# Linear attention and a bilinear feed-forward layer on one core: blocks of 128 tokens of all four rows instead of 256 tokens of two rows

## The chip, the cores and the metric

The kernel runs on one core of one Trainium2 chip. The time is device microseconds of one execution; the median of several is compared. Lower is better. "The profile" is the record of one execution by the hardware profiler, "the trace" is what it holds of single instructions, and `L787` is line 787 of the kernel before. Engines: PE is TensorE (PEld its weight loads), DVE is VectorE, ACT is ScalarE, POOL is GpSimd, SP is SyncE, which here only issues DMAs.

## The reference

For each of 4 rows and 8 heads a state of 48x48 runs over 768 tokens; each channel of the state decays by `alpha`. Its output goes through a bilinear feed-forward layer.

```python
q, k, v, alpha: (4, 8, 768, 48) float32, alpha in 0.8 to 1.0
state = np.zeros((B, H, D, D))
for t in range(S):
    state = alpha[:, :, t, :, None] * state + einsum('bhd,bhe->bhde', k[:, :, t], v[:, :, t])
    y[:, :, t] = einsum('bhd,bhde->bhe', q[:, :, t], state)
x = y.transpose(0, 2, 1, 3).reshape(3072, 384)
a = x @ w_a                 # (384, 1536)
b = x @ w_b
out = (a * b) @ w_out       # (1536, 384)
```

## The kernel before

**Blocks.** The work is cut into six blocks ("chunks", class `Chunk`), each of 512 tokens. Block `c` holds two rows (`b0 = c % 2 * 2`) and 256 tokens of each (segment `s = c // 2`). Its tiles put a pair of neighbouring tokens on a partition (`r` is which of the two), so 64 partitions are 128 tokens: `g` is the half of the partitions, the first or second 128 tokens, and `u` is which of the block's two rows.

**Steps of a block.** Each has a short name, which the table `OPS` at the end of the kernel maps to a function:

- `ld` (L519) loads alpha, keys, queries, values; the last argument names the issuing engine (Y is SP, P is POOL, S is ACT, V is DVE). `W` (L501) and `Wo` (L504) load the weights as bfloat16 through POOL. A load or step of `0a` or `0b` takes four of the eight heads of row `u` = 0.
- `ln` takes logarithms of alpha on ACT; `l2` (L533, DVE) adds the two tokens of each pair; `A` (L552) forms prefix sums over partitions by one fp32 matmul with a triangular matrix `ut`. Later blocks use `H`, `L` and `A2` (L572) for the same sum in two pieces. `E` (L594, ACT) takes exponentials of the sums with both signs (`beta`, `invb`).
- As the sums are for pairs, the first token of a pair has to be levelled: `ra` (L579, ACT) and `lv` (L586) multiply first-token keys by alpha and first-token queries by its inverse. `mk` and `mq` (L600, DVE) multiply keys and queries by the exponentials into `QKp`.
- `C` (L643) transposes by PE, `Ce` evicts the transposed tile; blocks 2 to 5 use the DMA transpose `T` (L654) instead. `D` (L709) makes scores, `M` (L714, DVE) masks them, or `Mc` (L718, ACT) copies and `Mm` (L722, DVE) masks. `v` casts values.
- `K` (L680) makes the update of the state on PE, `dk` and `de` (L622, L628) or `dr` and `dl` give the decay over a half, `k` (L694 to L698, DVE) applies both. `S0` holds states between segments, `Sm` those between the two halves of a segment.
- `SB` and `SA` add what the carried state gives to the output (L733, `carried`), `Y` adds the tokens within the block (L733, `inner`), `X` (L768) evicts the result as the feed-forward's input.
- Feed-forward: `a` and `b` (L787) for one of 12 slices of 128 and for a half (`0`, `1`) or all (`*`) of the block; `as` (L793) evicts `a` on ACT, `pr` (L801) multiplies on DVE, `o` (L809) and `oc` (L820) make the output, `ot` and `otc` evict, `st` and `stc` store.
- `fill` (L543) runs matmuls of zeros whose result nobody reads. `cu`, `ci`, `cm`, `cz`, `cs`, `c1`, `c1a` set up constants: triangular matrix, identity, masks, zero padding, zero states, ones, and ACT's function table.

**What sets the order.** All is written out by hand in the string `PROGRAM`: `0: ld a 0a Y` is step `ld` of block 0 with its arguments. Each engine runs its instructions in that order, and a DMA is issued in its issuing engine's order. The last number of many steps is the PSUM bank, eight in all; steps that name the same bank wait for each other. The loaded tiles and work tiles of a name have two buffers (`bufs`) or as many as is said.

Of the kernel before, what the change touches and what calls it, by code (L numbers as in the profile page):

```python
# [17 lines left out]
0: cu; ci; c1a; ld a 0a Y; cm 1; cz 0 q P; cs 1 0 P; c1; ld a 0b Y; fill 7 1; ld a 1 Y; ln 0a; cu2 P; ld q 0b P; ra 0a; fill 1 2; ln 0b; c2 P; ld v 0 P; ld v 1 P  # L18
0: l2 0a V; ld k 0b Y; A 0a 5; l2 0b V; ld q 1 P; ld q 0a Y; cs 0 m P; cm 0; E 0a b; ld k 0a Y; W b 0 256; ld k 1 Y; ra 0b; E 0a i; ln 1; fill 10 3; W a 256 768
0: cz 1 v V; l2 1 V; cz 0 b V; lv 0a q V; dk 3; A 0b 1; mq 0a V; fill 2 0; lv 0a k V; cs 0 0 V; mk 0a V; lv 0b k V; lv 1 k P; A 1 2; E 0b i; E 1 i; E 0b b  # L20
0: mk 0b V; de; E 1 b; C 0 0 5; lv 0b q V; v 0 S; fill 5 7; Ce 0 0 V; ra 1; D 0 0 2; mq 0b V; C 0 1 7; W a 0 256; M 0 0; K 0 0 0; Ce 0 1 S; fill 5 2; k 0 0 V
0: mk 1 V; SB 0 4; D 0 1 2; lv 1 q V; v 1 S; Mc 0 1; mq 1 V; Mm 0 1 V; K 1 1 6; K 1 0 7; k 1 0 V; K 0 1 1; C 1 0 0; Ce 1 0 S; cz 0 v P; Y 0; k 1 1 V; SA 0
0: X 0 S; k 0 1 V; W b 256 768
1: ld a 0 P; ld a 1 P
0: W a 768 1536; C 1 1 3; Ce 1 1 S; D 1 0 6; a 1 0 1; a 5 0 5; b 1 0 4; a 4 0 3; as 1 0; M 1 0; as 5 0; SB 1 6; D 1 1 1; a 3 0 5; W b 768 1536
1: ld k 0 P; ld q 0 P
0: as 4 0; b 5 0 3; pr 1 0; M 1 1; a 2 0 0; pr 5 0; cz 1 b P; as 3 0; b 2 0 4; b 4 0 5; pr 4 0
1: ld v 0 P
0: Wo 0 6; SA 1; Y 1; as 2 0; X 1 S
1: ld k 1 P  # L30
0: b 3 0 2; a 0 0 1; b 0 0 0; b 1 1 6; as 0 0; pr 2 0; pr 3 0; a 1 1 2
1: ln 0
0: a 2 1 4; b 0 1 5; a 4 1 1; as 1 1; b 4 1 7; pr 1 1; pr 0 0; as 2 1
1: ln 1
0: b 2 1 6; a 3 1 4; a 0 1 0; a 10 * 3
1: ra 0; l2 0 V
0: pr 2 1
1: l2 1 V
0: a 5 1 6; as 4 1; as 0 1
1: H 0 V  # L40
0: b 5 1 0
1: dk 1
0: as 5 1; Wo 6 12; pr 4 1; pr 5 1; a 9 * 6; b 11 * 0; cs 1 m P
1: lv 0 k P; H 1 S; ra 1; ld q 1 P; lv 0 q P
0: pr 0 1
1: L 0 V
0: as 10 *; cz 1 q V
1: de; A2 0 7
0: b 10 * 1
1: L 1 V  # L50
2: ld a * P
0: a 11 * 5; as 9 *; as 3 1; pr 10 *
1: A2 1 2
0: b 9 * 3; as 11 *; b 3 1 5
1: E 0 b; E 0 i
# [27 lines left out]
2: ln *  # L83
1: SA 0; Y 0
2: l2 * V
1: k 1 0 V
2: H * S
1: X 0 S; M 1 0; k 1 1 V
0: ot 0 S
# [866 lines left out]
```

## Time and profile before

| | |
|---|---|
| time, median of 3 runs | 199.71 us (198.07 to 200.48) |
| time of the profiled execution | 199.88 us |
| its span, first to last instruction | 197.8 us |
| PE busy | 188.0 us, 95% |
| DVE busy | 134.6 us, 68% |
| ACT busy | 106.0 us, 54% |
| POOL busy | 51.9 us, 26% |
| read from HBM, written | 25.98 MB, 4.74 MB |
| feed-forward matmuls (L787), busy | 56.2 us with w_b, 56.0 us with w_a |
| output matmuls (L809), busy | 49.4 us |

The profiled execution took 199.88 us, of which 197.8 us are its span. Busy times are sums per engine; an engine that is idle while another sets the end costs nothing. The clock that TensorE was granted stands at full speed in all slices of the page. The page's 40 slices are 4.9 us each; the DMA engines move 212 to 269 GB/s in slices 2 to 10 and 21 GB/s in slice 12.

### The profile page before, as it was taken

Reading aid. Unit: us, or ns where it says so; the run is one execution under the profiler, and the core shown is the slowest. Engines: PE = TensorE matmul, PEld = TensorE weight load, DVE = VectorE, ACT = ScalarE, POOL = GpSimd, SP = SyncE. Lnnn points to the kernel's source line nnn. Section 1 sums busy time; section 2 is a strip of 40 time slices with the busy share of each in tenths; the row PEclk is TensorE's granted clock in tenths of the full one; section 3 lists DMA queues with packets and bytes.
Section 4 is the critical chain, followed back from the end, with each engine's and each line's share of the span. In section 5 each row is a group of like instructions: output and inputs, shape, how many; then the busy total and the mean of one; then the engine's idle time right before and its main releaser. Section 6 shows DMA issues by size and latency. Waiting matters only on the chain.

```text
span 197.8 us, 6031 instructions
## 1 busy us (share of the span) xinstructions
PE 188.0 (95%) x2591; PEld 115.2 (58%) x2608; DVE 134.6 (68%) x223; ACT 106.0 (54%) x194; POOL 51.9 (26%) x70
## 2 busy tenths in 40 slices
PE   7877999999999999899999999999999999999993
PEld 2435886466788876644556644557555454545562
DVE  1599858886999989569778499955777524364311
ACT  5357686755699753196356566544435652334020
POOL 7989717681020206500005527000000000000000
PEclk9999999999999999999999999999999999999999
DMA  5999999999926999995999969500259100000224
GB/s 137 254 224 212 245 257 217 264 259 269 215 21 156 142 224 286 187 259 130 207 242 206 121 167 220 77 0 0 42 73 259 50 3 0 0 0 3 80 80 159
DMA packets 60282, 29.40 MB, mean 149 GB/s; under 512 B 51144, under 2 KB 58184, under 8 KB 60256
## 3 DMA queue, kind: packets, MB, share of 16 engines
q0 software_dynamic: 18688, 14.35, 40.4%
q1 hardware_dynamic: 41424, 14.57, 33.7%
q8 instruction: 20, 0.33, 0.7%
q10 hardware_dynamic: 144, 0.10, 0.2%
q14 instruction: 6, 0.05, 0.1%
HBM read 25.98 MB, written 4.74 MB: 155 GB/s over the span
## 4 chain that ended last, share of the span: by engine, by line
PE 83%; DMA 6%; DVE 5%; issue 2%; SPq 1%; ACT 1%; DVEq 0%; ACTq 0%
PE psum L787 42%; PE psum L809 23%; PE psum L733 7%; PE psum L709 4%; DMA kqT<-QKp 3%; DMA k_t<-in_k_dram 3%; PE psum L680 2%; PE psum L572 2%; DVE QKp L600 1%; SPq L519 1%; PE psum L643 1%; PE psum L820 1%; DVE prod L801 1%; DVE m L714 1%; PE psum L543 1%
## 5 line engine op out<-in xcount | busy, mean ns | idle before, releaser
L787 PE MATMUL psum<-xT,wb_t 128*128 128x512 bf16 (+1 forms) x264 | 56.2, 336 | 0.4 <-issue 0.2
L787 PE MATMUL psum<-xT,wa_t 128*128 128x512 bf16 (+1 forms) x261 | 56.0, 335 | 0.6 <-issue 0.2
L809 PE MATMUL psum<-wo_t,prod 128*128 128x384 bf16 x276 | 49.4, 326 | 0.1
L787 PEld LDWEIGHTS <-wb_t 128*128 128x128 bf16 x270 | 25.6, 98 | 19.3 <-issue 0.7
L809 PEld LDWEIGHTS <-prod 128*128 128x128 bf16 x276 | 26.2, 98 | 18.4 <-issue 0.2
L787 PEld LDWEIGHTS <-wa_t 128*128 128x128 bf16 x270 | 25.6, 98 | 19.1 <-issue 0.2
L718 ACT ACTIVATE m<-psum 128x1024 bf16<-128x1024 f32 x15 | 15.0, 1022 | 12.4 <-PE psum L709 12.4
L586 POOL TENSOR_TENSOR k_t<-k_t,a_t 128x384 f32<-128x384 f32 x8 | 8.5, 1064 | 40.2 <-issue 24.2
L600 DVE TENSOR_TENSOR QKp<-q_t,beta 128x768 bf16<-128x768 f32 (+1 forms) x13 | 12.2, 935 | 5.2 <-issue 2.9
L586 POOL TENSOR_TENSOR q_t<-q_t,ra 128x384 f32<-128x384 f32 x7 | 7.9, 1126 | 28.1 <-ACT ra L579 12.1
L824 ACT ACTIVATE ot<-psum 128x384 f32<-128x384 f32 (+1 forms) x13 | 6.1, 479 | 16.9 <-PE psum L809 14.4
L826 DVE COPY ot<-psum 128x384 f32<-128x384 f32 (+1 forms) x12 | 6.3, 535 | 10.6 <-PE psum L809 9.2
L768 ACT ACTIVATE xT<-psum 128x768 bf16<-128x768 f32 x9 | 7.3, 808 | 10.9 <-PE psum L733 10.8
L722 DVE TENSOR_TENSOR m<-m,mask 128x1024 bf16<-128x1024 bf16 x15 | 11.2, 748 | 1.8 <-ACT m L718 1.8
L714 DVE TENSOR_TENSOR m<-psum,mask 128x1024 bf16<-128x1024 f32 x9 | 11.0, 1221 | 1.3 <-PE psum L709 1.2
L600 DVE TENSOR_TENSOR QKp<-k_t,invb 128x768 bf16<-128x768 f32 (+1 forms) x13 | 11.4, 886 | 0.1
L733 PE MATMUL psum<-m,vx 64*64 64x128 bf16 x576 | 10.5, 217 | 1.1 <-DVE m L722 0.6
L526 ACT ACTIVATE la<-a_t 128x1536 f32<-128x1536 f32 (+2 forms) x9 | 9.5, 1058 | 2.7 <-DMA a_t<-in_alpha_dram 2.7
L709 PE MATMUL psum<-kqT 64*64 64x128 bf16 x384 | 9.9, 219 | 1.1 <-DVE kqT L651 0.9
L733 PEld LDWEIGHTS <-vx 64*64 64x64 bf16 x576 | 9.0, 107 | 2.2 <-issue 2.1
L543 PE MATMUL psum<-wz 128*128 128x512 bf16 x28 | 8.5, 440 | 1.8 <-DVE one L455 1.2
L533 DVE TENSOR_TENSOR l<-la 128x768 f32<-128x768 f32 (+2 forms) x9 | 6.2, 686 | 5.6 <-ACT la L526 5.6
(252 smaller groups left out, 278.8 us busy)
## 6 DMA issues: line engine op xcount, KB each, us to landing
out_dram<-ot SPq DMA_DIRECT2D x23, 192.0 KB, 3.1
a_t<-in_alpha_dram POOLq DMA_DIRECT2D x3, 768.0 KB, 9.8
q_t<-in_q_dram POOLq DMA_DIRECT2D x3, 768.0 KB, 11.5
k_t<-in_k_dram SPq DMA_DIRECT2D x3, 768.0 KB
v_t<-in_v_dram POOLq DMA_DIRECT2D x4, 384.0 KB, 8.7
q_t<-in_q_dram POOLq DMA_DIRECT2D x3, 384.0 KB, 9.7
wo_t<-in_moe_w_out_dram POOLq DMA_DIRECT2D x2, 576.0 KB, 15.2
v_t<-in_v_dram POOLq DMA_DIRECT2D x4, 192.0 KB, 8.8
```

Of the source, the lines that this page charges most:

```text
L526: nc.scalar.activation(out=ch.la[:, us, hs].rearrange("p b h r d -> p (b h r d)"), in_=ch.a[:, us, hs].rearrange("p b h r d -> p (b h r d) ...
L543: nc.tensor.matmul(bank(i), lhsT=wz[:, :C], rhs=wz, start=True, stop=True)
L586: eng.tensor_mul(x, x, by)
L600: eng.tensor_mul(QKp[ch.c % 2][:, u, j, :, hs, :D], src[:, u, hs].rearrange("p h r d -> p r h d"), by[:, u, hs].rearrange("p (o h) d -> p ...
L709: nc.tensor.matmul(s2[g * HC:(g + 1) * HC, r, p, rk, :], lhsT=ch.kqT[u][rs, 1, rk, 2 * h + p, g * HC:(g + 1) * HC], rhs=queriesT(ch, u, 2 ...
L714: nc.vector.tensor_mul(m.rearrange("p r a k s -> p (r a) (k s)"), ch.s2[u, h].rearrange("p r a k s -> p (r a) (k s)"), maskn(4))
L718: nc.scalar.activation(out=m.rearrange("p r a k s -> p (r a) (k s)"), in_=ch.s2[u, h].rearrange("p r a k s -> p (r a) (k s)"), func=AF.Copy)
L722: eng.tensor_mul(x, x, maskn(4))
L733: nc.tensor.matmul(y[c * DP:(c + 1) * DP, g, j // 2 * C:(j // 2 + 1) * C], lhsT=lhsT, rhs=rhs, start=(g, c) not in begun, stop=False, skip ...
L768: nc.scalar.activation(out=o_, in_=i_, func=AF.Copy)
L787: nc.tensor.matmul(p, lhsT=(wa_t, wb_t)[w][:, kk, f * 128:(f + 1) * 128], rhs=ch.xT[:, kk, us, :], start=(kk == 0), stop=(kk == KT - 1))
L809: nc.tensor.matmul(op, lhsT=ch.prod[:, f, at:at + C], rhs=wo_t[:, f, :], start=(f == 0), stop=(f == NFF - 1))
```

## The change

A block now holds 128 tokens of all four rows. `g` is a pair of rows (rows `2g` and `2g+1`) and `u` which of the two, so the two partition halves are different rows at the same tokens, and block `c` follows block `c-1` in every row. `Sm` is gone, and block 0 has no carried state, so its `Y` opens the output tile itself. A load covers one half of the partitions and its last argument says which; the two halves of a tile are loaded by two instructions, in part from two queues, and ACT issues loads too.

In block 0, `B` (`cum_both`) replaces `l2`, `ra`, `lv` and `A`: PE forms the prefix sums of both tokens of a pair by four fp32 matmuls, with `ut` and a shifted triangular matrix `uts`; the exponentials are taken for both tokens and lie in the buffer that the feed-forward's products use later. `dk` multiplies by a two-column matrix `og` in place of `one`, so that one matmul serves both halves. The order of the whole program is new.

The diff, cut to its core:

```diff
 PROGRAM = """
-0: cu; ci; c1a; ld a 0a Y; cm 1; cz 0 q P; cs 1 0 P; c1; ld a 0b Y; fill 7 1; ld a 1 Y; ln 0a; cu2 P; ld q 0b P; ra 0a; fill 1 2; ln 0b; c2 P; ld v 0 P; ld v 1 P
-0: l2 0a V; ld k 0b Y; A 0a 5; l2 0b V; ld q 1 P; ld q 0a Y; cs 0 m P; cm 0; E 0a b; ld k 0a Y; W b 0 256; ld k 1 Y; ra 0b; E 0a i; ln 1; fill 10 3; W a 256 768
...
+0: ld a 0a S 0; cm 0; cz 0 q V; c1; cz 0 b P; ld k 0a Y 0; ld a 0b S 1; ld q 0b P 0; cu; ci; ld k 0b P 1; ld a 0a Y 1; cz 1 q V; ld a 0b Y 0; ld k 0a S 1
+0: cu2 V; ld q 0a Y 1; ld q 0a S 0; cz 0 v P; cm 1; c1a; ld k 0b S 0; ld q 0b S 1; ld v 0 P 1; cus; fill 6 6; ld a 1 S 1; ln 0a; ld a 1 S 0; B 0a 6; ld q 1 Y 0
+0: ld k 1 S 1; ln 0b; ld v 0 P 0; ld k 1 Y 0; E 0a i; E 0a b; ld q 1 Y 1; B 0b 2; E 0b b; mk 0a V; ld v 1 P 0; E 0b i; W a 0 256; fill 5 0; mq 0a V; ld v 1 P 1
+0: mq 0b V; C 0 0 2; W b 0 256; mk 0b V; Ce 0 0 V; dk 0 4; C 0 1 5; W a 256 768; ln 1; D 0 0 0; B 1a 2; de 0; Ce 0 1 S; D 0 1 6; M 0 0; B 1b 4; E 1a b; M 0 1
+0: E 1a i; E 1b i; v 0 V
+1: ld a 1 P 0
+0: W b 256 768
+1: ld a 0 P 0; ld a 1 P 1; ld a 0 P 1
+0: E 1b b; mk 1a V; mk 1b V; Y 0 6; K 0 0 1; mq 1b V; X 0 S; k 0 0 V; mq 1a V; dk 1 2; W a 768 1536; C 1 1 5; a 1 0 3; Ce 1 1 V; C 1 0 6; v 1 S; Ce 1 0 V
+0: a 0 0 7; b 0 0 4; D 1 1 0; as 0 0; D 1 0 6; pr 0 0; as 1 0; M 1 1; Mc 1 0; Mm 1 0 V; b 1 0 3; a 4 0 5; a 3 0 4; a 5 0 0; as 4 0; de 1; pr 1 0; K 0 1 2
+0: Y 1 5; W b 768 1536; b 4 0 7; as 5 0; b 3 0 0; k 0 1 V; X 1 S; as 3 0; pr 3 0; b 2 0 1
...
-    one = cst.tile([C, 1], F32, name="one")
+    og = cst.tile([C, 2], F32, name="og")
+    uts = cst.tile([C, C], F32, name="uts")
-    Sm = [cst.tile([C, 2, D + P2 * VS], BF16, name=f"Sm{i}") for i in range(2)]
...
+    def const_uts():
+        x, y = (t.rearrange("p (g s) -> p g s", g=2) for t in (uts, ut))
+        nc.vector.memset(x[:, :, 0:1], 0.0)
+        nc.vector.tensor_copy(x[:, :, 1:], y[:, :, :HC - 1])
...
-    def load(ch, what, us, eng):
+    def load(ch, what, us, g, eng):
...
-        eng.dma_start(out=t[:, us, hs].rearrange("p b h r d -> p (b h) (r d)"),
-                      in_=src[ch.b0 + us.start:ch.b0 + us.stop, hs, ch.s * 2 * C:(ch.s + 1) * 2 * C, :].rearrange("b h (p r) d -> p (b h) (r d)", r=2))
+        eng.dma_start(out=t[g * HC:(g + 1) * HC, us, hs].rearrange("p b h r d -> p (b h) (r d)"),
+                      in_=src[2 * g + us.start:2 * g + us.stop, hs, ch.c * C:(ch.c + 1) * C, :].rearrange("b h (p r) d -> p (b h) (r d)", r=2))
...
+    def cum_both(ch, uh, i):
+        u, hs = uh[0].start, uh[1]
+        n = (hs.stop - hs.start) * D
+        ch.pf[u, hs.start, hs.stop] = p = wide(i)[:, :, :n]
+        x = ch.la[:, u, hs]
+        for r in range(2):
+            nc.tensor.matmul(p[:, r], lhsT=ut, rhs=x[:, :, 0, :], start=True, stop=False)
+            nc.tensor.matmul(p[:, r], lhsT=ut if r else uts, rhs=x[:, :, 1, :], start=False, stop=True)
...
     def expo(ch, uh, what):
...
+        if ch.c == 0:
+            if not hasattr(ch, "invb"):
+                x = wk.tile([128, NFF, NT], BF16, name="prod").rearrange("p f n -> p (f n)").bitcast(F32).rearrange("p (w u h r d) -> p w u h r d", w=2, u=2, h=H, r=2)
+                ch.invb, ch.beta = x[:, 0], x[:, 1]
...
-    def decay_pe(ch, tag):
+    def decay_pe(ch, us, tag):
...
+                xs = [ch.la[:, u, hd, rk, :] for rk in range(2)] if ch.c == 0 else [ch.l2[:, u, hd, :]]
+                for n, x in enumerate(xs):
+                    nc.tensor.matmul(s2[r * DP:r * DP + D, e:e + 2], lhsT=x, rhs=og, start=(n == 0), stop=(n == len(xs) - 1))
...
     def state(ch, us, g, eng):
-        old, mid, new = cut(S0[ch.s % 2], rows), cut(Sm[i], us), cut(S0[(ch.s + 1) % 2], rows)
-        src, dst = ((old, mid), (mid, new))[g]
+        rows = slice(2 * g + us.start, 2 * g + us.stop)
+        src, dst = cut(S0[ch.c % 2], rows), cut(S0[(ch.c + 1) % 2], rows)
...
-        row = (ch.b0 + m % 2) * S + (2 * ch.s + m // 2) * C
-        return out[row:row + C, :]
+        return out[m * S + ch.c * C:m * S + (ch.c + 1) * C, :]
...
-        "Y": lambda x, u: inner(x, int(u)),
+        "Y": lambda x, u, t=None: (t and out_tile(x, int(u), t), inner(x, int(u))),
```

In the later blocks the loads by half go out from POOL (42 loads in all, 23 before) and SP, block 1's four `lv` run on DVE where they ran on POOL, `K` and `k` are done for blocks 0 to 4 and not for block 5, and steps stand in other places and banks. At the end of the program both halves of the last output tile are evicted by ACT.

## The prediction

> **What bounds the kernel now** ("now" is the kernel before throughout). I first cut the span at the first feed-forward (FF) matmul and at the last matmul (windows over all engines: busy time and count of PE, PEld, DVE, ACT, POOL, then clock, DMA share and GB/s).
>
> ```profile
> core 0: us, PE busy (x) PEld busy (x) DVE busy (x) ACT busy (x) POOL busy (x), PEclk, DMA share, GB/s
> 0.00:21.30 21.30, 16.48 (x302) 9.56 (x305) 13.52 (x28) 11.99 (x22) 19.33 (x39) 1.00 1.13 214
> 21.30:194.70 173.40, 171.53 (x2293) 105.68 (x2304) 121.12 (x195) 93.69 (x172) 32.54 (x32) 1.00 0.71 141
> 194.70:197.80 3.10, 0.00 (x0) 0.00 (x0) 0.00 (x0) 0.33 (x1) 0.00 (x0) 1.00 0.37 123
> ```
>
> From 21.3 us on PE is the bound: 171.53 of 173.40 us busy, so new orders can win at most 1.9 us there, and the tail is 3.1 us. In the first 21.3 us PE is also called busy, but 8.5 us of that are the filler matmuls of L543. The room is here. The chain of waits in this stretch says what sets it (start, us, what):
>
> ```profile
> 3.74 6.17 DMA k_t<-in_k_dram
> ...
> 14.51 1.24 DVE m L714
> ...
> 17.60 1.03 ACT m L718
> 18.65 0.70 DVE m L722
> ...
> 19.40 1.03 PE psum L733 x54
> ...
> 21.33 1.47 PE psum L787 x12
> ...
> 25.05 0.95 PE psum L733 x54
> ```
>
> The fourth load on SP holds the keys until 9.9 us; then keys, queries, transpose, scores and two masks follow one another, until L733 (`Y 0`) can run at 19.40 and L787 (FF) at 21.33. The second `Y` ends at 26.0. Last, the timeline of the same stretch and of the tail, for prices (start, us, engine, line, out<-in, count):
>
> ```profile
> 0.73 1.28 ACT L451 ACT_TABLE_LOAD   x1 [0.73 <-PEq L940]
> 0.74 1.56 SPq L519 DMA_DIRECT2D a_t<-in_alpha_dram  x3
> 1.19 3.33 PE L543 MATMUL psum<-wz 128*128 128x512 bf16 x8 [1.19 <-DVE one L455]
> 3.53 0.52 ACT L526 ACTIVATE la<-a_t 128x384 f32<-128x384 f32 x1 [1.51 <-DMA a_t<-in_alpha_dram]
> 3.74 2.59 SPq L519 DMA_DIRECT2D k_t<-in_k_dram  x2
> 4.99 2.32 PE L543 MATMUL psum<-wz 128*128 128x512 bf16 x10
> 9.97 0.81 PE L552 MATMUL psum<-l,ut 128*128 128x384 f32 x2
> ```
>
> ```profile
> 195.08 0.37 ACTq L845 DMA_DIRECT2D out_dram<-ot  x1
> ```
>
> A DMA issue costs ACT 0.37 us (96 KB); on SP it costs 0.52 us, and 1.30 us when the loads pile up. The first logarithm starts at 3.53. Fillers take 0.42 us each at first and 0.23 us from 4.99 on.
>
> **The change, part by part.** *PE's total.* `Y`, scores and FF keep their counts. Cross and own carries: before, blocks 0 and 1 have half each, now block 0 none and block 1 all: 120 matmuls both ways. `K`: ten halves both ways (block 5 needs none now, block 4 two). `dk` in block 1 falls from 64 rows (0.90 us) to 32: -0.45 us. State updates on DVE: 6+6+4+4+2+2 before, 4+8+4+4+4 after, the same. Weights are no earlier or later in bytes. So the end moves by what the front moves.
>
> *Issue on ACT.* Nine half loads now go through ACT's queue, seven and the table load ahead of the first logarithm, two more between it and the second. Behind them wait the logarithms, and on these every prefix sum. I take 0.40 us each (ACT's own row of the same 96 KB, with its gap): 0.73 + 7x0.40 + 1.28 = 4.8 for `ln 0a`, 1.3 us later than now; with 0.52 us it ends 5.35; two issues and 0.52 more: `ln 0b` ends 6.65. The other end is 1.30 us an issue (SP's row), kept below as a rival. Alpha itself is there: now 192 KB land by 3.53.
>
> *Prefix sums.* `l2`, `ra` and the levelling go in block 0: DVE loses three instructions of L533 (0.36+0.36+0.56) and five of L586 (0.35 to 1.16 each), ACT three of L579 (0.36+0.35+0.51). For each half row pair PE adds four fp32 matmuls of 192 columns for one of 192; 768 columns are two of the 0.81 us groups: 1.6 us. So `B 0a` 5.35-6.95, `B 0b` to 8.55. The exponentials double to 0.49 us (128x384 row): `E 0a` both by 8.0, `E 0b` 8.6-9.6. Their cover is PE's empty front. The shifted matrix (`cus`) is two small DVE instructions before 4 us, hidden behind the loads.
>
> *Keys and queries.* k 0a now stands first on SP and third on ACT, so L600 waits for the exponentials: four multiplications of 0.55 us, two at 7.5-8.6, two at 9.1-10.2. POOL issues k 0b's half at about 3.9; +5.0 us (shortest landing of L519) is 8.9, in time. Five fillers at 0.22 us, `C 0 0` to 10.25 (now it starts at 11.35), eviction on DVE 0.70 to 10.95, `dk` 0.5, `C 0 1` to 11.35, ACT's eviction 1.02 to 12.4, `D 0 0` to 11.8, mask on DVE 1.23 to 13.05. PE then does `B 1a` (1.6) before `D 0 1`: 13.85; mask to 15.1, values cast 0.35 to 15.45. `Y 0` 15.45-16.4 instead of 19.40. `X 0` 0.81 to 17.2; `C 1 1` waits for DVE's three multiplications to 17.1, so the first FF group starts at 17.7, 3.6 us earlier.
>
> *To the second `Y`.* Evictions of both transposes on DVE to 19.4; three FF halves (0.33 us each by the rows at 25.94 to 27.26), scores to 20.0 (the second needs the bank that `as 0 0` empties, behind `v 1`), masks to 21.8, four more halves and `K 0 1` beside them: `Y 1` 21.8-22.75, where it now ends at 26.0: 3.2 us. But 7 halves are done where now there are 9: -0.66; `K 1` is still to do, -0.55; `dk` +0.45. Net 2.4 us.
>
> *Loads of the rest.* POOL gets 42 loads where it has 23, at 0.9 us each. By its rows the weights go out at 9.5, 11.2, 12.0, 13.7, 17.2 and 18.0; now 9.81 to 17.80. The last 576 KB land 11.6 us later (L501's slowest), 29.6; PE asks for them at 30.7. Block 1's queries go out by 23.4; with the 12.4 us of today's k_t (18.57 to 30.97) minus the 0.9 us of their issue they are in by 34.9, transposed form wanted at 37.5, after 0.55 and 0.95 us on DVE: 0.6 us to spare. Four levellings of block 1 go from POOL (1.0 us) to DVE (0.55 us): 2.2 us between 30 and 50 us, where DVE is idle 4.2 us (busy 4.11+4.28+7.44 of 20). SP's later half loads (12 for 5 whole ones, 0.4-0.5 us each) stand ahead of transposes and stores; L654's two waits for transposes are 1 us in all now. I cost these at nothing, covered by those margins; if a margin is gone, the overrun is PE's wait.
>
> Sum: 199.88 (profiled execution; span 197.8 and 2.1 around it) - 2.4 = 197.5; the profile is 0.17 above the median of 199.71: **197.3 us**.
>
> [...] The clock: eight fillers ran at 0.42 us before ten at 0.23 came, 3.8 us after the first. Now six start at about 1.7 (DVE clears the padding first), 2.6 us of work, then PE is idle for a microsecond. By the row's 3.8 us `B 0a` is just warm; cold it costs 1.6 us more. I take 0, because the row counts from the first filler; ends 0 and 1.6. [...]
>
> Loads by halves: in 5 to 10 us the core already gets 254 GB/s, and no slice of the page shows over 286, so I take no faster landing. [...]
>
> **Rivals.** *Bigger front gain.* If four chained fp32 matmuls cost 1.0 us, not 1.6 (L552's rows are 0.33 to 0.49 and overlap), three of them lie on the path and give 1.8; the orders win half of the 1.9 us idle; the late weights take 0.7 back: 197.3-2.0 = 195.3. For it: PE's front is a pure chain. Against: weights at 29.6.
>
> *The loads give it back.* Landing times of L519 spread from 5.0 to 14.3 us. With 14.3 for block 1's queries PE waits 1.3 us, with the weights late too all 2.4 go: 199.7. This is also the case that halves from two queues land no sooner than whole loads. Against: DMA bytes ahead of them are fewer than now.
>
> *ACT's queue becomes the front (slower).* At SP's piled-up 1.30 us, three issues ahead of `ln 0a` and two ahead of `ln 0b` cost 0.9 more each: 4.5 us, of which 4.2 reach `E 0b`: 201.5, slower than before. It decides from 0.9 us an issue on (2.4/5 + 0.4); over 203.7 from 1.8 us.
>
> **How the numbers follow.** Chances: forecast 0.36 (own range 195.8 to 199), bigger gain 0.32, given back 0.13, ACT's queue 0.19, of this 0.12 over 203.7. About 2% either way, 195.7 and 203.7, is what a measurement can tell from no change. Faster 0.32, same 0.36+0.13+0.07 = 0.56, slower 0.12. The range goes from the bigger gain with all of the 1.9 us and the first group a microsecond earlier still (193.5) to ACT's queue at 1.4 us (202), leaving 0.2 out.
>
> **What would show it.** Right: `Y 0` (L733) starts near 15.5, the first FF group near 17.7, second `Y` ends near 22.8, 2.4 us of lead stay to the last matmul. `ln 0a` after 6 us, or ACT rows of issue over 0.9 us, speak for the slow rival; FF waits on wb_t or block 1's transposes behind q_t for the loads. A first FF group after 20 us, or PE idle for over 3 us after it, makes the prediction wrong.

## The result, and the profile after

The changed kernel takes 211.57 us (median of 4 runs, 210.14 to 213.01); the kernel before takes 198.89 us beside it. The ratio is 1.066, with a 95% interval of 1.054 to 1.079. The forecast was 197.3 us with a range up to 202.0: it missed by 14 us and had the sign wrong. The profiled execution took 211.11 us, its span is 209.1 us. Where single executions of a kernel lie over 1.5% above its fastest one, the ratios and intervals below leave them out, and the medians do not.

The first view is the cut that the prediction began with: windows over all engines of the changed kernel, cut at the first feed-forward (FF) matmul and at the end of the FF work (columns as there: busy time and count of each engine, then clock, DMA share, GB/s).

```profile
0.00:22.90 22.90, 17.53 (x227) 13.51 (x228) 9.45 (x22) 9.35 (x17) 16.02 (x35) 1.00 1.18 187
22.90:206.00 183.10, 174.03 (x2345) 107.04 (x2357) 124.56 (x208) 96.36 (x176) 35.52 (x45) 1.00 0.81 136
```

The reader should see three things. The first FF matmul is not earlier but 1.6 us later (22.9 against 21.3). The stretch behind it grew by 9.7 us (183.1 against 173.4): PE now idles 9.1 us there, where it idled 1.9, and is busy 2.5 us more. The tail, 206.0 to 209.1, is the same 3.1 us. So of 11.3 us more span, some 7 are new waits *after* the front, which is where the prediction had put nothing; 5.7 us of PE's idle time lie between 90 and 122 us, where it is busy 26.29 us of 32.00.

The next view answers to the chain of waits in the front (start, us, what).

```profile
2.14 4.41 DMA k_t<-in_k_dram
...
6.58 0.60 ACTq L546
...
7.23 0.53 ACT la L553
...
20.60 0.85 PE psum L775 x46
...
23.10 0.33 PE psum L827 x3
...
27.85 1.73 issue
```

The chain still begins with the landing of a key load, but that load now holds ACT: `ln 0a` (L553) starts at 7.23 us, where the logarithm started at 3.53 before. `Y 0` (L775) starts at 20.60 instead of 19.40, and the first FF group (L827) near 23 instead of 21.33. The last line is a wait of 1.73 us in the second `Y` for which the profile names no releaser.

How a load can hold ACT shows in ACT's timeline of the changed kernel (start, us, engine, line, form, count, idle time before it and what ended it).

```profile
0.74 1.37 ACTq L546 DMA_DIRECT2D a_t<-in_alpha_dram  x2
...
5.84 0.60 ACTq L546 DMA_DIRECT2D q_t<-in_q_dram  x1
6.58 0.60 ACTq L546 DMA_DIRECT2D a_t<-in_alpha_dram  x1
7.23 0.52 ACT L553 ACTIVATE la<-a_t 128x384 f32<-128x384 f32 x1 [2.46 <-DMA k_t<-in_k_dram]
```

Each issue costs 0.60 to 0.71 us, and the sixth began only at 5.84, 1.1 us after the table load had ended (4.76). In the chain above the seventh (6.58) is released by the landing of a key load (2.14 + 4.41). The logarithm stands behind seven of them.

On PE, the same stretch of the changed kernel:

```profile
1.73 2.74 PE L570 MATMUL psum<-wz 128*128 128x512 bf16 x6 [1.73 <-DVE og L476]
7.80 1.01 PE L587 MATMUL psum<-la,ut 128*128 128x192 f32 x2 [3.33 <-ACT la L553]
...
17.31 0.49 PE L588 MATMUL psum<-la,uts 128*128 128x192 f32 x2
```

Six fillers, then 3.33 us of nothing, then prefix sums whose pairs follow each other every 0.64 us; the same pairs at 17.31 follow every 0.33 us. So `B 0a` and `B 0b` ran cold, which here means at half the rate. The page's clock row shows full clock there, but the trace's clock records begin only at 13.97 us, at full clock, and the page shows full clock where there is no record. In the trace of the kernel before they begin at 4.13 us, about where its fillers go from 0.42 to 0.23 us each.

The last view is the row of bytes moved in 40 slices, from the page of the changed kernel and then from that of the kernel before.

```profile
GB/s 116 208 187 215 216 219 177 207 216 198 187 190 193 196 111 210 184 187 218 182 170 189 161 188 153 173 24 3 3 88 192 117 38 3 0 0 39 3 113 150
```

```profile
GB/s 137 254 224 212 245 257 217 264 259 269 215 21 156 142 224 286 187 259 130 207 242 206 121 167 220 77 0 0 42 73 259 50 3 0 0 0 3 80 80 159
```

The same 29.40 MB move, but slices 2 to 10 carry 177 to 219 GB/s where they carried 212 to 269, and the slices in which the kernel before had caught up with its loads (21 GB/s in slice 12) are gone. In the DMA records a 384-byte packet on SP's queue takes 35 ns (median) instead of 22, and POOL's packets of 4224 bytes take 360 instead of 254. So the time per byte has grown by 59% for the first and by 42% for the second.

### The profile page after: what moved, and what is told of

It is laid out like the page before. It is cut to its first block, busy times and chain, and to the rows that moved or that the text cites. A ratio compares the mean times of both kernels' runs of the same rounds, so it can differ in the third digit from the quotient of the medians.

```text
span 209.1 us, 6050 instructions
## 1 busy us (share of the span) xinstructions
PE 191.7 (92%) x2568; PEld 120.5 (58%) x2583; DVE 134.0 (64%) x230; ACT 106.1 (51%) x193; POOL 51.5 (25%) x79
## 2 busy tenths in 40 slices
DMA packets 61143, 29.40 MB, mean 141 GB/s; under 512 B 52182, under 2 KB 59254, under 8 KB 61116
## 4 chain that ended last, share of the span: by engine, by line
PE 73%; DMA 13%; issue 6%; SPq 3%; DVE 1%; ACT 1%; ACTq 1%; DVEq 0%
PE psum L827 38%; PE psum L849 16%; PE psum L775 5%; DMA a_t<-in_alpha_dram 5%; DMA kqT<-QKp 4%; PE psum L751 3%; PE psum L724 2%; DMA k_t<-in_k_dram 2%; DMA q_t<-in_q_dram 2%; PE psum L687 2%; PE psum L587 2%; PE psum L588 2%; SPq L546 1%; PE psum L667 1%; PE psum L608 1%
## 5 line engine op out<-in xcount | busy, mean ns | idle before, releaser
L827 PE MATMUL psum<-xT,wb_t 128*128 128x512 bf16 (+1 forms) x262 | 56.0, 336 | 1.8 <-ACT as__1809 L833 1.0
L827 PE MATMUL psum<-xT,wa_t 128*128 128x512 bf16 (+1 forms) x263 | 55.8, 336 | 1.0 <-ACT as__1840 L833 0.7
L827 PEld LDWEIGHTS <-wa_t 128*128 128x128 bf16 x270 | 25.5, 98 | 21.1 <-issue 2.0
L827 PEld LDWEIGHTS <-wb_t 128*128 128x128 bf16 x270 | 25.7, 98 | 20.5 <-issue 2.1
L760 ACT ACTIVATE m<-psum 128x1024 bf16<-128x1024 f32 x14 | 14.2, 1022 | 14.1 <-PE psum L751 14.1
L775 PE MATMUL psum<-m,vx 64*64 64x128 bf16 x576 | 11.0, 217 | 5.2 <-issue 2.5
L756 DVE TENSOR_TENSOR m<-psum,mask 128x1024 bf16<-128x1024 f32 x10 | 12.2, 1221 | 5.5 <-PE psum L751 5.5
L553 ACT ACTIVATE la<-a_t 128x1536 f32<-128x1536 f32 (+2 forms) x9 | 9.5, 1055 | 7.9 <-DMA a_t<-in_alpha_dram 4.3
L775 PEld LDWEIGHTS <-vx 64*64 64x64 bf16 x576 | 9.1, 107 | 7.1 <-issue 7.1
L546 POOL DMA_DIRECT2D v_t<-in_v_dram x16 | 12.3, 778 | 1.4 <-issue 0.6
L622 POOL TENSOR_TENSOR q_t<-q_t,ra 128x384 f32<-128x384 f32 x4 | 4.0, 1005 | 35.0 <-DMA q_t<-in_q_dram 20.3
L646 DVE TENSOR_TENSOR QKp<-q_t,beta 128x768 bf16<-128x768 f32 x10 | 9.4, 952 | 1.0 <-ACT beta L636 0.9
L646 DVE TENSOR_TENSOR QKp<-k_t,invb 128x768 bf16<-128x768 f32 x10 | 9.5, 951 | 0.4
L764 DVE TENSOR_TENSOR m<-m,mask 128x1024 bf16<-128x1024 bf16 x14 | 9.5, 682 | 0.0
L622 POOL TENSOR_TENSOR k_t<-k_t,a_t 128x384 f32<-128x384 f32 x3 | 3.0, 1006 | 26.5 <-DMA out_dram<-ot 15.2
L751 PEld LDWEIGHTS <-kqT 64*64 64x64 bf16 x384 | 6.4, 106 | 5.1 <-issue 2.6
L587 PE MATMUL psum<-la,ut 128*128 128x192 f32 x16 | 5.7, 450 | 3.3 <-ACT la L553 3.3
## 6 DMA issues: line engine op xcount, KB each, us to landing
wo_t<-in_moe_w_out_dram POOLq DMA_DIRECT2D x2, 576.0 KB, 10.7
```

The costliest lines, as they stand in the source:

```text
L546: eng.dma_start(out=t[g * HC:(g + 1) * HC, us, hs].rearrange("p b h r d -> p (b h) (r d)"), in_=src[2 * g + us.start:2 * g + us.stop, hs, ...
L553: nc.scalar.activation(out=ch.la[:, us, hs].rearrange("p b h r d -> p (b h r d)"), in_=ch.a[:, us, hs].rearrange("p b h r d -> p (b h r d) ...
L587: nc.tensor.matmul(p[:, r], lhsT=ut, rhs=x[:, :, 0, :], start=True, stop=False)
L646: eng.tensor_mul(QKp[ch.c % 2][:, u, j, :, hs, :D], src[:, u, hs].rearrange("p h r d -> p r h d"), f)
L751: nc.tensor.matmul(s2[g * HC:(g + 1) * HC, r, p, rk, :], lhsT=ch.kqT[u][rs, 1, rk, 2 * h + p, g * HC:(g + 1) * HC], rhs=queriesT(ch, u, 2 ...
L756: nc.vector.tensor_mul(m.rearrange("p r a k s -> p (r a) (k s)"), ch.s2[u, h].rearrange("p r a k s -> p (r a) (k s)"), maskn(4))
```

## The experiments

Three theories stood after this. *Halves*: a load that writes only 64 partitions moves its bytes slower, and everything that waits for bytes is late. *Count*: the number of loads (issues, descriptors, ACT's queue) is the cost. *Front and order*: the cold prefix sums ("warm" below is the full rate, a pair of matmuls every 0.33 us) and the new in-order places on SP and DVE are the cost, and the slow bytes only follow. Below, "lag" is how much later than in the kernel before the same share of the FF and output matmuls is done, read off the two traces.

**The halves taken out of the change, the halves put into the kernel before, the count put into the kernel before, and more fillers.** Four kernels on one chip, where the kernel before takes 198.81 us.

`after_spread` writes all 128 partitions with each load, half of the heads (or one of two rows) at a time. Queue, place, size and packets of every load stay; the tokens in a block are others than the reference's.

```diff
-        eng.dma_start(out=t[g * HC:(g + 1) * HC, us, hs]..., in_=src[2 * g + us.start:2 * g + us.stop, hs, ch.c * C:(ch.c + 1) * C, :]...)
+        if us.stop - us.start == 2:
+            us = slice(us.start + g, us.start + g + 1)
+        else:
+            w = (hs.stop - hs.start) // 2
+            hs = slice(hs.start + g * w, hs.start + (g + 1) * w)
+        eng.dma_start(out=t[:, us, hs]..., in_=src[ch.c % 2 * 2 + us.start:ch.c % 2 * 2 + us.stop, hs, ch.c // 2 * 2 * C:(ch.c // 2 + 1) * 2 * C, :]...)
```

> The changed kernel with every load instruction kept at its place, on its queue and at its size, but each spread over all 128 partitions and half of the heads (or one of two rows) instead of 64 partitions. It loads other tokens of the same inputs, so what is computed is not the reference; the work is the same. Theory A (a load into half of the partitions moves its bytes slower, and the loads then starve the front and blocks 3 and 4): packets of 384 bytes on SP fall back from 35 ns towards 22 ns, the 20 to 40 us stretch moves 240 to 260 GB/s again, and the time falls from 211.6 to 199 to 204 us. Theory B (issue on ACT, cold prefix sums and the new orders cost the time, the loads are a symptom): 209 to 212 us. Theory C (twice as many DMAs is what costs): 209 to 212 us, as their number is unchanged.

Measured: ratio 1.036 (1.027 to 1.045), from two executions of 205.31 and 206.18 us; with two at 210.54 and 210.95 us the median is 208.36. In the profiled execution, that of 210.54 us, packets on SP are back at 22 ns, ACT's issues at 0.37 to 0.52 us, `ln 0a` at 6.03, the first FF matmul at 20.97. That is 3 of the 6.6 points of the loss, not all of it.

`before_half` is the kernel before with each load cut in two by partition half, both on the load's own queue:

```diff
-        eng.dma_start(out=t[:, us, hs]..., in_=src[..., hs, ch.s * 2 * C:(ch.s + 1) * 2 * C, :]...)
+        for g in range(2):
+            eng.dma_start(out=t[g * HC:(g + 1) * HC, us, hs]..., in_=src[..., hs, (ch.s * 2 + g) * C:(ch.s * 2 + g + 1) * C, :]...)
```

> The kernel before with every load issued as two DMAs on the same queue, one for each half of the partitions. Theory A: DMA-bound stretches go from about 245 to about 205 GB/s, the front's keys land 1 to 2 us later and the time rises by 4 to 10 us, to 203 to 209. Theory B: at most +2 us for the added issues. Theory C: +4 to +10 us, but then the split by heads costs as much.

Measured: 211.87 us, ratio 1.064 (1.056 to 1.072); packets at 35 ns; lag 8.7 us at the first FF matmul, 13.9 us from 86 us on, in a profiled execution that took 213.79 us. One edit to the loads alone costs as much as the whole change.

`before_heads` cuts the same loads in two by heads or by row, so that each piece writes all 128 partitions:

```diff
-        eng.dma_start(out=t[:, us, hs]..., in_=src[ch.b0 + us.start:ch.b0 + us.stop, hs, ...]...)
+        n, w = us.stop - us.start, (hs.stop - hs.start) // 2
+        for g in range(2):
+            ug = slice(us.start + g, us.start + g + 1) if n == 2 else us
+            hg = hs if n == 2 else slice(hs.start + g * w, hs.start + (g + 1) * w)
+            eng.dma_start(out=t[:, ug, hg]..., in_=src[ch.b0 + ug.start:ch.b0 + ug.stop, hg, ...]...)
```

> The kernel before with every load issued as two DMAs on the same queue, both over all 128 partitions, each half of the heads (or one of the two rows). Theory A: 199 to 202 us, only the added issues on POOL and SP. Theory B: the same. Theory C: +4 to +10 us, as for halves of the partitions.

Measured: 200.73 us, ratio 1.011 (1.005 to 1.018); packets at 22 ns, no lag. *Count* is worth 1.1% here. With the same number of loads, halves cost 5 points more (1.064 against 1.011): *count* falls as the main cause.

`after_fill` is the changed kernel with `fill 20 6` for `fill 6 6`.

> The changed kernel with 20 instead of 6 filler matmuls ahead of the first prefix sum, so that PE is busy until the first logarithm is there. If the two prefix sums took 2.6 us each because PE's clock had not risen, they now take 1.3 us each and the first feed-forward matmul comes 1.5 to 2.6 us sooner. Theory A: the loads are late behind it, so 209.5 to 211.5 us. Theory B: the gain stays to the end, 208.5 to 209.5 us.

Measured: 211.75 us, ratio 1.062 (1.053 to 1.071), the same as the changed kernel. `B 0a` and `B 0b` now run warm, 7.98 to 10.6 us instead of 7.80 to 13.0, and the gain is lost at once: the second row's logarithm waits for its alpha until 14.9, and the first FF matmul is no earlier (23.25). PE pauses 1.59 us for it at 14.2, and from 15.89 to 19.30 us its granted clock is 0.50, so that `B 1a` runs at half the rate (its pairs at 0.64 us again). With the bytes late, the faster PE in front bought nothing here (ratio 1.062 against 1.066).

**What a half load costs by itself.** `load_rates` has none of the reference's work: six phases read the same 4.72 MB, and a copy on DVE (L53) waits for the last byte of each. It was executed once. The cut shows the function for a half and phase 4.

```python
    def half(n, g, eng):
        eng.dma_start(out=big[g * HC:(g + 1) * HC, n]..., in_=src[n % 3][n // 3 * 2:n // 3 * 2 + 2, :, g * C:(g + 1) * C, :]...)
...
    for n in range(6):
        half(n, 0, nc.sync)
        half(n, 1, nc.scalar)
    done()
```

> Loads alone, none of the reference's work: six phases, each of which reads the same 4.7 MB of alpha, keys and queries in packets of 384 bytes, with a copy by VectorE between them: 1, whole loads over 128 partitions on SP; 2, the same as two loads by row, 128 partitions, on SP; 3, as two loads by partition half, lower and upper in turn, on SP; 4, the lower half on SP and the upper half on ACT's queue; 5, by row, one on SP and one on ACT's queue; 6, all lower halves on SP and then all upper halves. If a load into 64 partitions moves slower because of the partitions that it reaches: 1, 2 and 5 take 18 to 22 us, 3 and 6 take 1.3 to 1.7 times as long with packets near 35 ns instead of 22, and 4 is back near the time of 1 if both halves are really under way at once. If the number of loads were the cost: 2 as slow as 3. If halves cost nothing by themselves: all six within 10%, and the slow packets of the changed kernel come from its mixture with stores and weights.

DVE's timeline of it; the number in brackets is the wait for the phase's last byte:

```profile
39.83 4.96 DVE L53 CAST got<-big 128x9216 bf16<-128x9216 f32 x1 [16.95 <-DMA big<-in_q_dram]
69.42 4.96 DVE L53 CAST got<-big 128x9216 bf16<-128x9216 f32 x1 [24.64 <-DMA big<-in_q_dram]
92.57 4.96 DVE L53 CAST got<-big 128x9216 bf16<-128x9216 f32 x1 [18.19 <-DMA big<-in_q_dram]
...
144.99 4.96 DVE L53 CAST got<-big 128x9216 bf16<-128x9216 f32 x1 [25.23 <-DMA big<-in_q_dram]
```

These are phases 2, 3, 4 and 6; phase 5 waited 17.26 us. Loads over all partitions take 17 us whether cut by row (16.95) or by row over two queues (17.26); the whole loads of phase 1 took 17.2 from their first issue. Halves in turn on one queue take 24.64, all lower and then all upper halves 25.23: 1.45 and 1.49 times as long, with packets of 36 and 39 ns for 22. Lower and upper halves under way at once from two queues take 18.19, packets at 22 ns again. Phases 3, 4 and 6 issue the same twelve loads from the same addresses, so neither the loads' number nor where they read is the cause. The slow phases are those in which one queue carried both halves, in turn or one kind after the other. Opposite halves from two queues gain 24.64/18.19, or 35%, over the same halves in turn on one queue.

**Both causes taken out together.** `spread_fill` is `after_spread` with `fill 20 6`. It ran, with `load_rates`, `after_order` and `before_B` below, where the kernel before takes 200.48 us.

> The changed kernel with its loads over all 128 partitions (as in after_spread, so with other tokens in the blocks) and 20 fillers instead of 6. If the cold TensorE in the first prefix sums is the rest of the front's loss: the four pairs per sum go at 0.33 us instead of 0.64, both sums end near 9.2 instead of 11.2 us, the first FF matmul starts at 18.5 to 19.5 us instead of 20.97, and the time is 1.5 to 2 us under after_spread, 203.5 to 206.5. If the landing of keys and queries is the limit there as well, as it was in after_fill: the first FF at 20.5 or later and the same time as after_spread within 0.7 us.

Measured: 205.44 us, ratio 1.027 (1.022 to 1.032). PE's timeline of it:

```profile
1.73 6.28 PE L575 MATMUL psum<-wz 128*128 128x512 bf16 x20 [1.73 <-DVE og L476]
...
17.55 0.86 PE L780 MATMUL psum<-m,vx 64*64 64x128 bf16 x48 [0.19 <-DVE vx L717]
...
19.88 0.49 PE L832 MATMUL psum<-xT,wa_t 128*128 128x256 bf16 x3
```

With whole-width loads and a warm PE the front does what the change meant: `Y 0` at 17.55 against 19.40, first FF at 19.88 against 21.33. The fillers now end last: `ln 0a` is done at 6.34, and `B 0a` starts behind them at 7.85; whether fewer fillers would win more was not tested. The filler that gained nothing with late bytes (`after_fill` against the changed kernel) shortens `B 0a` and `B 0b` to 2.6 us here; the two ratios (1.036 and 1.027) have intervals that touch, so its worth in the whole time, some 1.8 us, is not established. Against `after_fill` (1.062) the only edit is the shape of the loads: 3.5 points, some 7 us.

**The later orders.** `after_order` is the changed kernel with block 4's loads on SP issued earlier, and block 4's two `lv` behind block 3's last mask.

```diff
+3: l2 * V
+4: ld a * Y 0; ld a * Y 1
...
-4: ra 0
+4: ra 0; ld q * Y 0; ld q * Y 1; ld k * Y 0
...
-4: A2 0 5; lv 0 k V
+4: A2 0 5
...
-4: E 0 b; lv 0 q V
-3: Mm 0 1 V; Y 1; SA 1
+4: E 0 b
+3: Mm 0 1 V
+4: lv 0 k V; lv 0 q V
+3: Y 1; SA 1
```

> The changed kernel as it is, loads by halves included, with block 4's loads of alpha, queries and keys issued earlier on SP and its two level multiplications on VectorE put behind the last in-place mask of block 3. If the later order is what costs 4 to 5 us between 85 and 122 us: the waits of TensorE at 91 (2.0 us) and at 119 us (2.5 us) go away and the time is 207 to 208 us. If the bytes are late whatever the order (the loads by halves fill the queues): the waits come back elsewhere, and the time is 210.5 us or more.

Measured: 228.32 us, ratio 1.140 (1.134 to 1.145). Neither theory had this. A line of SP's timeline and, in the second fence, one of the chain tell why:

```profile
106.31 1.32 SPq L545 DMA_DIRECT2D q_t<-in_q_dram  x2
```

```profile
104.47 1.82 DVE QKp L645 x2
```

Block 5's queries are loaded ahead of block 4's and take the buffer that block 2's have left, so block 4's take that of block 3's queries. Moved up, the load stands on SP from 89 us, waits until block 3's last multiplication on DVE (104.47) and holds block 3's own decay rows and transposes behind it. The edit was a bad test of the orders; it shows that SP executes its list in order, at 17 us for one load put too early.

`after_order2` moves no load: only DVE's order changes, in block 4 as above, and in block 2, where `lv 0 k`, `mk 0` and `mq 0` go up behind those of the second row.

```diff
-2: v 1 V
+2: mq 0 V; v 1 V
...
-2: mk 1 V
+2: mk 1 V; lv 0 k V; mk 0 V
```

> The changed kernel with VectorE's order alone changed in two places, no load moved: block 2's three multiplications for the first row (lv 0 k, mk 0, mq 0) right behind those of the second row, and block 4's two level multiplications behind the last in-place mask of block 3. If the in-order wait at 119 us is what it looks like, it goes away (2.5 us) and the time is 208.5 to 209.5 us; the earlier turned tile of block 2 adds at most 1 us more, since in the changed kernel the wait at that place is small. If the late bytes are what counts: within 1 us of the changed kernel.

Measured, where the kernel before takes 200.06 us: 210.24 us, ratio 1.053 (1.043 to 1.063), against 1.066 (1.054 to 1.079) for the changed kernel; the intervals overlap. The wait that it aims at is real. In the changed kernel's chain:

```profile
111.24 4.17 DMA q_t<-in_q_dram
115.41 4.43 issue
119.84 0.06 DVE k_t L622
...
120.32 0.55 DVE q_t L622
120.87 0.61 DVE m L764
...
121.53 1.03 PE psum L775 x60
```

Two `lv` of block 4 (L622) stand ahead of a mask of block 3 (L764) on DVE, and DVE idles 4.43 us ahead of the first of them, for nothing that the profile names (SP issues a load of block 4's keys at 111.94), and the mask's `Y` (L775) waits 2.4 us on PE. With the order changed the lag at 120 us is 9.2 us instead of 11.6. At 130 us it is 10.7, against 11.2 in the changed kernel: PE now waits 1.3 us at 134.5 for block 4's transposed tile instead. So most of what this wait gave back is gone at the next one.

`after_opp` takes `fill 20 6` and changes only which half goes on which queue in block 0's loads: there SP carries upper halves alone and ACT lower halves alone.

```diff
-ld a 0a S 0; ... ld k 0a Y 0; ld a 0b S 1; ld q 0b P 0; ... ld a 0b Y 0; ld k 0a S 1
+ld a 0a S 0; ... ld k 0a Y 1; ld a 0b S 0; ld q 0b P 1; ... ld a 0b Y 1; ld k 0a S 0
...
-ld q 0b S 1; ... ld a 1 S 1; ... ld q 1 Y 0; ... ld k 1 S 1; ... ld k 1 Y 0
+ld q 0b S 0; ... ld a 1 Y 1; ... ld q 1 S 0; ... ld k 1 S 0; ... ld k 1 Y 1
```

> The changed kernel with 20 fillers (as after_fill) and, in blocks 0's loads, other halves on the same queues: SP's queue carries upper partition halves only and ACT's lower halves only, so that the two queues that are under way together always write opposite halves; in the changed kernel they often write the same one. load_rates gives 18.2 us for opposite halves at once, 24.6 for one queue with halves in turn and 17.2 for whole loads. If that is what slows the front: packets of 384 bytes come back to 22 to 27 ns before 20 us, ln 0a starts before 6.5 us, the first FF matmul at 20 to 21.5 us against 23.2 in after_fill, and the time is 208 to 210 us against 211.75. If it is not the halves' meeting but ACT's issues or the later loads: first FF after 22.5 us, time within 1 us of after_fill.

Measured: 209.49 us, ratio 1.048 (1.039 to 1.056). The first FF matmul comes at 20.92 instead of 23.25 in `after_fill`, and ACT's packets stay at 22 ns until 8 us (between 4 and 8 us 31 ns in `after_fill`, 29 in the changed kernel). SP's are at 32 ns there, for 33 and 34, and from 8 us on all are at 35 to 38 ns. So pairing the halves goes with an earlier front, by one profile of each, but most packets stay slow, and why SP's do was not tested. The intervals of the two ratios touch (`after_fill` 1.053 to 1.071).

`after_opp_order2` is both together.

> after_opp and after_order2 together. If front and order are separate losses, both gains add: 2 to 3 us in front and 2 to 3.5 us at 76 and 119 us, together 206 to 207.5 us, still over the kernel before, because the later blocks' loads by halves on one queue stay. If one gain is eaten by the next wait: 208 us or more.

Measured: 212.50 us, ratio 1.062 (1.054 to 1.070): the gains do not add; the second of the two expectations holds. First FF at 20.2, lag 1.2 us soon after it, 9.6 us by 86 us: PE waits 1.9 us at 66.8 and 3.7 us at 83.2.

**The new prefix sums alone, with whole loads.** `before_B` puts the sums of both tokens and the decay from `la` into block 0 of the kernel before and takes out `l2`, `ra`, `lv` there. All loads stay whole.

```diff
-0: cz 1 v V; l2 1 V; cz 0 b V; lv 0a q V; dk 3; A 0b 1; mq 0a V; fill 2 0; lv 0a k V; ...
+0: cz 1 v V; cz 0 b V; mq 0a V; E 0b b; mk 0a V; E 0b i; cs 0 0 V; mk 0b V; C 0 0 5; mq 0b V; dk * 3; de *; B 1 6; E 1 i; E 1 b
```

> The kernel before with one part of the change alone: block 0's prefix sums of both tokens by TensorE (and its state decay from the logarithms), so that the pair sums, the ratios and the level multiplications of block 0 go away; all loads, blocks and later orders stay as they were. If the prefix sums are worth what the prediction put on them: the last keys of block 0 land at 9.96 us as before, then VectorE has only mk, mk, mq and the eviction ahead of the mask, so Y 0 starts near 16.4 us instead of 19.40, the first FF matmul near 18.5 instead of 21.33, and the time is 196 to 197 us. If what is gained in front is lost again to the weights or to a later wait: 198.5 or more. If the new sums are themselves the loss: over 200.

Measured: 202.74 us, ratio 1.012 (1.008 to 1.017): 1.2% slower. `before_B2` puts the first scores ahead of the second row's sums and drops five fillers.

```diff
-... C 0 0 5; mq 0b V; dk * 3; de *; B 1 6; E 1 i; E 1 b
-0: v 0 S; fill 5 0; Ce 0 0 V; D 0 0 1; C 0 1 4; W a 0 256; M 0 0; ...
+... C 0 0 5; mq 0b V; dk * 3; C 0 1 4; Ce 0 0 V; D 0 0 1; B 1 6; Ce 0 1 S; M 0 0; de *
```

> before_B with TensorE's order in front mended: in before_B TensorE did the state decay (1.56 us) and the second row's sums (2.8 us) ahead of the first scores, which began only at 16.45 us although the transposes' eviction had ended at 12.1 us. Here the transposes of both head halves and the first scores stand ahead of the second row's sums, and the idle fillers between them are gone. If TensorE's own time for the sums was what ate the gain: the first scores at 12.3 to 13.5 us, the first FF matmul at 19 to 20.5 us instead of 21.33 in the kernel before, and the time 1 to 2 us under the kernel before. If the gain is lost whatever the order: the first FF at 21 us or later and a time within 1% of the kernel before or over it.

Measured: 200.99 us (10 runs), ratio 1.006 (1.002 to 1.010). PE's timeline of `before_B2`:

```profile
11.26 1.63 PE L649 MATMUL psum<-og,la 128*48 128x2 f32 x64
...
13.37 0.42 PE L735 MATMUL psum<-kqT 64*64 64x128 bf16 x16
13.72 0.91 PE L569 MATMUL psum<-la,ut 128*128 128x384 f32 x2
```

The levelling is gone from DVE, but the decay (L649, 1.6 us) and the second row's sums (L569 and L570, 2.8 us) now stand among transposes and scores, ahead of the second scores. `before_B3` moves them under the loads, before 11.8 us.

```diff
-... W a 256 768; B 0b 1; fill 10 7
+... W a 0 256; W a 256 768; B 0b 1; dk 0 3; B 1 6
```

> The kernel before with the new prefix sums in block 0 alone, as before_B2, in an order that lets TensorE do the second row's sums (2.6 us) and half of the decay in the time before the keys land (9.96 us), where before_B2 had 2.3 us of fillers, and that puts the second row's exponentials on ScalarE ahead of the eviction instead of ahead of the second mask. If the sums are worth what the prediction said once TensorE's time for them lies in the shadow of the loads: Y 0 at 16.4 to 17 us (19.40 in the kernel before), the first FF matmul at 18.7 to 19.5 us (21.33), the time 197.5 to 198.5 us where the kernel before gives 200. If the front is not what sets the end, or the weights or block 1's loads are not there by then: the first FF is early and the time the same as before within 0.7 us.

Measured, where the kernel before takes 200.43 us: 203.33 us, ratio 1.015 (1.008 to 1.022). `Y 0` starts at 17.39, 2 us earlier than in the kernel before, but the first FF matmul comes at 22.9. The windows of its PE (length, busy and count, granted clock, DMA share, GB/s) say where it went:

```profile
15.00:18.00 3.00, 2.29 (x79) 0.74 1.25 207
18.00:21.00 3.00, 3.00 (x95) 0.50 1.14 287
21.00:24.00 3.00, 3.00 (x39) 0.62 1.13 219
```

PE was granted half its clock from 16.44 to 23.27 us (the windows cut this stretch in three), and eight transposes took 0.97 us instead of 0.55. This is no accident of one execution: all six of `before_B3` have a mean clock of 0.974 to 0.988, those of the kernel before beside them 0.991 to 1.0, and those of `before_B2` 0.997 to 1.0. A likely cause is in the edit itself. It drops the fillers that the kernel before has between 11.8 and 17 us, and PE pauses there, in its timeline:

```profile
14.46 0.43 PE L705 MATMUL psum<-vx,QKp 64*64 64x48 bf16 x16 [1.05 <-ACT vx L691]
15.49 0.24 PE L758 MATMUL psum<-kqT,Sm 64*64 64x128 bf16 x2 [0.60 <-DVE Sm L719]
```

In other traces, too, the clock falls at pauses of PE (last section). None of the three kernels is faster than the kernel before. Whether the sums would gain 2 us with the pauses filled is open; no run shows it.

**What remains.** `spread_order2` is `spread_fill` with DVE's order of `after_order2`.

> spread_fill (loads over all partitions, 20 fillers) with after_order2's two changes of VectorE's order. In spread_fill TensorE waits 2.3 us at 74 us for the second turned tile of block 2, whose multiplications VectorE did at 66.5 to 69 us, 3 us later than the kernel before does its own. If that order is what remains of the loss once the bytes arrive in time: the wait goes, the lag behind the kernel before at 85 us falls from 4.3 to 2 us or less, and the time is 202.5 to 204 us against 205.4. In the changed kernel itself the same edit only moved the wait (1.4 us at 70 us in its place), which the late bytes would explain. If it moves here too: over 204.7 us, and the order is not the rest.

Measured: 205.55 us, ratio 1.028 (1.021 to 1.035): no gain over `spread_fill`. The wait for the transposed tile at 74 us is gone, and two others take its place; the longer one, in the chain of `spread_order2`:

```profile
81.64 2.31 issue
```

PE waits 2.3 us in a `Y` for nothing that the profile names, and at 65 us 1.8 us for a product on DVE (the moved multiplications stand ahead of it, until 66.3 us). The theory that this order is the rest falls.

## Why the prediction was wrong

**The step that failed** is the one costed at nothing: "I take no faster landing" for the halves, and the later loads at "nothing, covered by those margins". I asked whether halves from two queues land *sooner*, and bounded the other side by 2.4 us. The 254 and 286 GB/s given as the reason are of the kernel before, whose loads write all 128 partitions; they bound a gain and say nothing of a loss. That a split costs no more than its issues was my estimate, which no run had shown: in `load_rates` the same bytes took 24.64 us by halves in turn and 16.95 us by row, both on one queue. The measured price is 3.5 points, some 7 us, in this change (`after_fill` against `spread_fill`), which is about half of the loss, and 5 points in the kernel before (`before_half` against `before_heads`).

*PE's stretch after the first FF.* The prediction gave new orders at most the 1.9 us of idle time to win and never asked how much idle time they could add. It became 9.1 us. The margins that were to cover the later loads were 0.6 and 1.1 us (the figures given for the queries come to 1.1 as well; where the 0.6 is from is not said). They were reckoned from the old landing times, and at 30 us the lag is already over 4 us. POOL's half loads are 43, not 42.

*Issue on ACT*: 0.40 us each predicted, 0.60 to 0.71 measured, and the sixth held back by another 1.1 us. `ln 0a` was at 7.23, not 4.8, past the 6 us that was to speak for the slow rival. That rival had the place right and its price wrong: the issues stayed below its 0.9 us, and the chain's delay there came from a landing. With whole-width loads the issues cost 0.37 to 0.52 and `ln 0a` starts at 5.82 to 6.03, so about 1.3 us of the 2.4 us came from the halves.

*Prefix sums*: 1.6 us each predicted, 1.3 us each when warm (`spread_fill`), 2.6 us each in the changed kernel, cold. The warm-up was weighed and taken at 0, counted from the first filler, and that count did not carry over. In the kernel before the eight fillers were busy for 3.33 us, and the clock records, at full clock, begin 2.9 us after the first of them; here the six were busy for 2.74 us, a pause of 3.33 followed, and the records begin 6.2 us after the first prefix sum. With twenty fillers (6.28 us, `spread_fill`) the sums ran warm; how few would do was not tested. But even those 2.6 us for both sums are worth nothing while alpha and the keys are late (`after_fill`).

*Net front gain*: 3.6 us at the first FF predicted, 1.5 us in `spread_fill`, -1.6 us in the changed kernel. In the prediction the sums removed DVE's work and cost PE nothing because "their cover is PE's empty front". `before_B2` shows that the front is empty only up to the landing of the keys at 9.9 us; behind it the sums and the decay stand between the transposes and the second scores.

*The rivals.* "The loads give it back" looked at the right place, late landings, and gave them 2.4 us at most, for block 1's queries and the last weights. It did not ask whether the bytes themselves move slower, and they did on SP's, ACT's and POOL's queue. *The chances*: the 0.12 for slower by over 2% is all from ACT's queue, as the loads were bounded at 199.7 us.

*What stays open.* With whole-width loads and a warm PE, 2.7% (2.2 to 3.2) are still lost. In the profile of `spread_fill` PE idles 4.1 us behind the first FF (1.9 before), 2.1 us of it a wait for a transposed tile at 74 us. Right behind that wait, from 77.07 us, the granted clock is 0.50 for 3.41 us, by my estimate 1.7 us of PE (half of it). Work that the kernel before does ahead of its first FF and this one behind it (a group of transposes, one of scores and three state halves: 0.55, 0.42 and 0.73 us by its rows) is the third part. With the 1.5 us won in front these come to 4.1 of the 4.4 us between the two spans. That is an account of one profile, not a test; the one test of it (`spread_order2`) moved the waits and gained nothing. The number of loads can be a part of these 2.7% too: it cost the kernel before 1.1% (`before_heads`), and no run takes it out of the change.

## What to carry to other kernels

A load that writes half of the partitions should be priced by its bytes, at a rate measured for it, and not only by its issue (24.64 us against 16.95 for the same bytes in `load_rates`): in this kernel the layout of a block decided the loads' shape, and that cost more than the layout won. When a change touches how bytes arrive, set the prediction's bounds by making *every* later landing slower by one factor and asking where the first margin ends, before counting any gain in front. Loads that a computing engine issues ahead of its own first work stand in its way: `ln 0a` came at 5.82 us instead of 3.53 even with whole-width loads. Moving a step earlier on an in-order queue needs the date at which its buffer comes free (`after_order`, 228.32 us against 211.57).

## What the runs showed of the hardware that was not expected

- In `load_rates` packets of 384 bytes take 22 ns where the loads cover all partitions, and 36 to 39 ns where one queue carries halves, in turn or one kind after the other; opposite halves from two queues are back at 22 ns and 18.19 us for 4.72 MB.
- The issue of a load got slower there as loads piled up, and slower still with slow bytes: the first load's issue took SP 0.44 us, and from the third on one took 2.35 to 2.53 us (768 KB); two halves in turn together took 3.53 to 3.70 us.
- In nine of the traces the granted clock falls to 0.50 for a while although there is work (`after_fill`, `after_opp`, `after_opp_order2`, `after_order`, `after_spread`, `before_half`, `before_B3`, `spread_fill`, `spread_order2`); the mean clock of these profiled executions is 0.962 to 0.992, that of the kernel before 1.000. Three of them: in `after_fill` 3.41 us from 15.89 on, behind a pause of 1.59 us; in `spread_fill` 3.41 us from 77.07 on, behind a pause of 2.1 us at 74; in `before_B3` 6.83 us from 16.44 on, behind two short pauses of 1.05 and 0.60 us. So a wait on PE cost more than itself there: half of 3.41 us is, by my estimate, another 1.7 us. Not every pause did it: 2.36 us at 119 us in the changed kernel did not.
- At the start these traces have no clock record until about where the matmuls reach their full rate: the first is at 4.13 us in the kernel before, at 13.97 in the changed kernel and at 11.17 in `after_spread`, where the pairs of `B 0b` pass from 0.64 to 0.33 us at 11.2. The full clock that a page or window shows ahead of them shows nothing.
- Waits of PE named only "issue" (1.73 us in the changed kernel, 2.31 us in `spread_order2`) begin within a microsecond of a transfer of the instruction queue (26.9 and 81.5 us in the DMA records). There are 20 such transfers in the 209 us of the changed kernel, most of them without such a wait. Whether the two belong together was not tested.
